# Decay attention and a gated convolution: one key tile transposed on TensorE, and another order of the same steps

## The chip, the cores and the metric

The kernel runs on one core of a Trainium2 chip. The metric is the device time of one execution in microseconds (us). Before the change it is 206.38 us (median of 3 runs, 206.31 to 206.44).

## The reference

There are two parts, in float32 throughout. The first is linear attention with a decay: 4 batches, 8 heads, 768 positions, head size 64. Written for blocks of 64 positions, with `Dmask[i,j] = lam**(i-j)` for j <= i:

```python
intra = (qb @ kb.T * Dmask) @ vb                  # inside a block
inter = (qb * lam**(pos+1)) @ kv_state            # what earlier blocks left
out   = intra + inter
kv_state = lam**64 * kv_state + (kb * lam**(63-pos)).T @ vb
```

Its output, laid side by side over the heads, is x, with 512 columns. The second part is `out = (sigmoid(conv5(x)) * (x @ w_val)) @ w_out`, where conv5 is a causal convolution of 5 taps for each column, and both matrices are 512 x 512.

## The kernel before

**Tiles.** Two batches go together, and 128 positions make a chunk, so there are 12 chunks (0 to 5 are the first pair of batches, 6 to 11 the second). Every chunk has two loads of 1 MB on SyncE's queue: `ld.i.0` brings q and k with head columns on the partitions (qT, kT; buffers lq0 to lq2), `ld.i.2` brings v and k with positions on the partitions (buffers lv0 to lv2).

**Steps of a chunk i.** `s.i` (TensorE): scores from kT and qT; chunks 0 to 2 have them in two halves, `s.i.0` and `s.i.1`. `m.i.*` (VectorE, DVE): scores times the decay mask, out of PSUM into buffer A. `ia.i` (TensorE): A times v into the PSUM tile xp; there is one such tile (xp0, two banks) for all chunks. `in.i` (TensorE): the share of the state. `kd.i`: k times its decay, in place in the lv tile, on ScalarE (ACT) for the chunks in K_ACT and on GpSimd (POOL) else. `st.i` (TensorE): k times v, into PSUM. `up.i` (DVE): the new state. `fd.i` (POOL): the faded state for the next chunk. `qd.i` (POOL): q times its decay. `x.i`, `xh.i` (ACT) and `xl.i` (DVE for chunks 0 and 1, POOL else): x out of xp, split in a high and a low part for the products of higher precision. xp0 comes free for the next chunk when these have read it.

**Steps of the second part.** `t.*`: the five taps (one on ACT, four on DVE), `sg`: the sigmoid, `v` and `V`: 12 matmuls each for x @ w_val, `ap`, `hh`, `hl`: the gate and the split of the product, `p`: x @ w_out, `ev`, `o`: out of PSUM and to memory.

**Weights.** w_val, w_out and conv_w come as 64-bit floats. `wv.0`, `wv.1`, `wo.0`, `wo.1` load 1 MB each and `cv` loads 20 KB; the steps `.e .n .s .w .v` (DVE), `.r .m .h` (ACT) and `.l` (POOL) make a high and a low 32-bit part of them. `dm` (DVE, L216) makes the decay mask, `dc` (ACT, L237) cuts it to blocks, `qe` (POOL) makes the decay of q. `f.0` (L206) is a matmul of zeros that computes nothing. Nine such matmuls of zeros (L188) stand at the start.

**Order.** ORDER is a list of all steps, written out. `Plan.run` issues them in that order; each engine runs its own steps one after the other, and SyncE issues the DMAs in that order too. A name after the colon is the buffer that a step takes.

Of the kernel before, what the change touches and what calls it, by code (L numbers as in the profile page):

```python
# [37 lines left out]
wv.0.1.w wv.0.1.v wv.0.1.h ld.3.2:lv1 wv.1.0.n s.2.0:s0 wv.1.1.e:val3 s.2.1:u1,u2 up.1.0 xh.1 wv.0.1.l v.0.1
m.2.0.0:A0 m.2.1.0 wv.1.0.m:u0 xl.1 wv.1.0.w wv.1.0.r hi.0 pb.0.0:val0 m.2.0.1:A1 wv.1.0.s cv.e qd.2.0:qd1 wv.1.0.v
qd.2.1 wv.1.1.n x.1 wv.1.1.r cv.r s.4.0:s0 cv.n v.1.0:u3 v.1.1 wv.1.0.h wv.1.1.s wv.1.1.m:u0 m.2.1.1 wv.1.1.w wv.1.1.v  # L40
ia.2.0:xp0 ia.2.1 wv.1.0.l cv.m m.4.1.0:A0 kd.2.0 wv.1.1.h fd.1.0 wo.0.0.n:val1 cv.s in.2.0 x.2:x1 pb.1.0:val2
wv.1.1.l m.4.0.0 st.2:u1 wo.0.0.e wo.0.0.r up.2.0 qd.4.0:qd0 cv.w cv.v xh.2:xs1 wo.1.1.e:val3 t.0.0.0:u2,g0 s.3.0:s0
xl.2.0 wo.0.0.m:u0 v.0.2:u3 m.3.0.0:A1 ld.6.2:lv2 v.0.3 pb.0.1 t.0.0.1 kd.3.0 t.0.0.2 xl.2.1 t.0.0.3 wo.0.0.w qd.4.1
ld.5.0:lq2 wo.0.0.s t.0.0.4 v.1.2:u1 sg.0.0 qd.3.1:qd1 v.1.3 v.2.2:u3 v.2.3 pb.1.1 wo.1.1.n fd.2.0 wo.0.0.v m.3.1.0
wo.1.1.m:u2 wo.1.1.r ld.6.0:lq0 st.3:u0,u1 wo.0.0.h qd.3.0 ia.3.0:xp0 in.3.0 wo.1.1.w wo.1.1.s wo.1.1.v wo.0.0.l hi.1
s.5.0:s0 kd.4.0 v.2.0:u2 up.3.0 in.3.1 wo.0.1.e:val1 wo.0.1.r fd.3.0 wo.1.1.h wo.0.1.n wo.0.1.m:u0 wo.0.1.s wo.1.1.l
up.3.1 fd.3.1 ia.3.1 v.2.1 x.3 xh.3 xl.3.1 ia.4.0:xp0 t.0.1.0:u1 ld.5.2:lv1 wo.0.1.w xl.3.0 pb.2.0:val3 m.5.1.0:A1
m.5.0.0 wo.0.1.v pb.2.1 wo.0.1.h wo.0.1.l s.6.0:s0 st.4:u0,u2 qd.5.1:qd1 kd.6.0 t.0.1.1 t.0.1.2 t.0.1.3 in.4.0 up.4.0
fd.4.0 t.0.1.4 sg.0.1 v.3.0:u3 kd.5.0 v.3.2:u0 qd.5.0 in.4.1 ia.4.1 ld.7.2:lv0 t.0.3.0:u1 t.0.3.1 up.4.1 t.0.3.2
x.4:x2 t.0.3.3 t.0.2.0:u2 kd.5.1 v.3.3 pb.3.1:val1 t.0.2.1 t.0.2.2 xh.4:xs0 ld.7.0:lq1 ia.5.0:xp0 in.5.0 t.0.2.3  # L50
fd.4.1 st.5:u0 up.5.0 v.3.1 pb.3.0 t.0.3.4 xl.4.1 in.5.1 sg.0.3 t.0.2.4 ap.1.0 ap.0.0 sg.0.2 ap.1.1 xl.4.0
wo.1.0.e:val2 wo.1.0.r v.4.0:u0 v.4.2:u3 wo.1.0.n wo.1.0.m:u1 ap.0.1 v.4.1 wo.1.0.s hh.1.1:hs0 wo.1.0.w pb.4.0:val0
hh.1.0 hl.1.1 wo.1.0.v m.6.1.0:A0 v.4.3 m.6.0.0 t.1.1.0:u2,g1 t.1.1.1 wo.1.0.h ia.5.1 st.6:u0,u1 up.6.0 x.5 s.7.0:s0
ia.6.0:xp0 hl.1.0 p.1.1.0.0:u0 t.1.1.2 hh.0.1:hs1 hh.0.0 t.1.1.3 pk.6 wo.1.0.l p.1.1.0.1 pb.4.1 qd.6.1:qd0 t.1.1.4
qd.6.0 t.1.3.0:u3 sg.1.1 t.1.3.1 t.1.3.2 t.1.3.3 t.1.3.4 ev.1.1.0:o0 o.1.1.0 xh.5 in.6.1 hi.2 ia.6.1 p.1.0.0.0:u2
fd.6.0 x.6:x0 t.1.0.0:u0 hl.0.0 sg.1.3 hl.0.1 p.1.0.0.1 up.6.1 ld.11.2:lv1 t.1.0.1 t.1.0.2 t.1.0.3 t.1.0.4
p.0.1.0.0:u1 ev.1.0.0:o1 p.0.1.0.1 t.1.2.0:u3 m.7.0.0:A1 t.1.2.1 t.1.2.2 t.1.2.3 m.7.1.0 sg.1.0 xl.5.0 p.0.0.0.0:u2
p.0.0.0.1 xl.5.1 v.5.0:u0 ld.8.0:lq2 t.1.2.4 ev.0.1.0:o2 o.1.0.0 xh.6:xs1 qd.7.0:qd1 t.2.3.0:u1,g0 v.5.1 ap.3.0
ld.8.2:lv2 ev.0.0.0:o0 sg.1.2 pb.5.0:val2 ap.3.1 ap.2.0 qd.7.1 kd.7.1 ia.7.0:xp0 in.7.0 kd.7.0 ap.2.1 hh.2.1:hs0
st.7:u2,u3 fd.6.1 v.5.2:u0 v.5.3 hh.2.0 t.2.3.1 t.2.3.2 up.7.0 s.8.0:s0 in.7.1 t.2.3.3 t.2.1.0:u2 t.2.3.4 hh.3.0:hs1  # L60
ia.7.1 hh.3.1 hl.2.0 sg.2.3 pb.5.1 p.2.0.0.0:u1 t.2.0.0:u0 t.2.1.1 ld.9.2:lv0 t.2.1.2 t.2.0.1 fd.7.0 up.7.1 hl.2.1
t.2.0.2 t.2.0.3 kd.8.0 p.2.0.0.1 ev.2.0.0:o1 t.2.0.4 sg.2.0 p.2.1.0.0:u3 kd.8.1 t.2.2.0:u1 t.2.1.3 p.2.1.0.1 t.2.1.4
o.2.0.0 sg.2.1 m.8.0.0:A0 o.0.0.0 t.2.2.1 t.2.2.2 t.2.2.3 t.2.2.4 ev.2.1.0:o1 o.0.1.0 ap.4.0 ap.5.0 ld.9.0:lq0 hl.3.1
hi.3 hl.3.0 x.7 p.3.0.0.0:u0 p.3.0.0.1 p.3.1.0.0:u2 t.3.0.0:u3,g1 xh.7 p.3.1.0.1 o.2.1.0 ia.8.0:xp0 sg.2.2 ap.4.1
t.3.0.1 hh.4.0:hs0 t.3.0.2 t.3.0.3 qd.8.1:qd0 fd.7.1 qd.8.0 in.8.0 ev.3.0.0:o0 hl.4.0 hh.4.1 hl.4.1 ev.3.1.0:o2
t.3.0.4 st.8:u1,u0 up.8.0 xl.6.0 ap.5.1 p.4.0.0.0:u2 m.8.1.0 t.3.1.0:u1 xl.7.1 p.4.0.0.1 fd.8.0 in.8.1 t.3.1.1 t.3.1.2
ia.8.1 t.3.1.3 ev.4.0.0:o1 o.4.0.0 ld.10.0:lq1 s.9.0:s0 m.9.1.0:A1 p.4.1.0.0:u2 sg.3.0 x.8:x1 p.4.1.0.1 xl.6.1
# [15 lines left out]
t.5.2.0:u3 o.8.0.0 apw.5.1 hhw.5.1:hs1 t.5.2.1 t.5.2.2 p.9.1.0.1 ev.9.1.0:o2 t.5.2.3 t.5.2.4 sg.5.2 o.7.1.0 V.5.0:u1
hlw.5.1:val1 V.5.3:u0 apw.5.0 o.9.1.0 apw.5.3 hhw.5.3 hlw.5.3:val3 p.8.1.0.0:u2 p.8.1.0.1 V.5.2:u3 hhw.5.0 ev.8.1.0:o0
o.8.1.0 hlw.5.0 p.10.1.0.0:u0 o.6.0.0 apw.5.2 hhw.5.2 hlw.5.2 p.11.1.0.0:u1 p.11.0.0.0:u2 p.11.0.0.1 ev.11.0.0:o2
o.11.0.0 p.11.1.0.1 ev.11.1.0:o0 o.11.1.0 p.10.1.0.1 ev.10.1.0:o1 o.10.1.0 p.10.0.0.0:u3 p.10.0.0.1 ev.10.0.0:o2
o.10.0.0 p.11.1.1.0:u2 p.11.1.1.1 ev.11.1.1:o0 o.11.1.1
# [815 lines left out]
```

## Time and profile before

| | |
|---|---|
| median of 3 runs | 206.38 us |
| the profiled execution's own time | 206.52 us |
| its span, first to last instruction | 204.7 us |
| TensorE (PE) busy | 197.6 us, 97% |
| DVE busy | 154.1 us, 75% |
| ACT, POOL busy | 114.3 and 115.4 us |
| read from HBM | 29.38 MB |

Times in the profile count from the first instruction, so a span is about 1.8 us shorter than the execution's own time. Busy time of PE overlaps between matmuls that follow each other, and the end of a matmul is modelled; how long a step holds TensorE is read from the start of one step to the start of the next. SPq are DMA issues of SyncE. In a row of the timeline the brackets give the engine's idle time before the row, and what ended it.

### The profile page before, as it was taken

The numbers are of one execution on the slowest core, as the hardware profiler recorded it, in microseconds if no ns is written. First come the engines' busy times: TensorE is split into PE (matmuls) and PEld (weight loads), VectorE is DVE, ScalarE is ACT, GpSimd is POOL, SyncE is SP. The second block draws the span as 40 slices with busy tenths as digits, with TensorE's granted clock in tenths as the row PEclk, the third lists the DMA queues.
The fourth block names the chain that finished last, engine by engine and source line by source line (L and its number), as shares of the span: only waits on it lengthen the run. The fifth ranks groups of instructions, "written<-read, shape, count | busy, mean of one in ns | idle before, by whom it ended". The sixth has DMA issues, their size and how long they took to land.

```text
span 204.7 us, 7451 instructions
## 1 busy us (share of the span) xinstructions
PE 197.6 (97%) x3312; PEld 171.6 (84%) x3312; DVE 154.1 (75%) x240; ACT 114.3 (56%) x218; POOL 115.4 (56%) x113
## 2 busy tenths in 40 slices
...
GB/s 175 426 429 419 422 424 423 421 360 27 195 51 362 8 3 118 373 232 3 297 297 29 203 400 122 3 3 152 8 106 0 0 3 102 102 51 14 93 127 78
DMA packets 7952, 36.15 MB, mean 177 GB/s; under 512 B 1136, under 2 KB 1392, under 8 KB 4336
## 3 DMA queue, kind: packets, MB, share of 16 engines
...
q8 instruction: 26, 0.43, 0.9%
q14 instruction: 6, 0.05, 0.1%
HBM read 29.38 MB, written 6.29 MB: 174 GB/s over the span
## 4 chain that ended last, share of the span: by engine, by line
PE 87%; DMA 9%; SPq 2%; issue 0%; ACT 0%; ACTq 0%
PE op L841 33%; PE vp L732 33%; DMA lq<-in_qkv 9%; PE xp L510 5%; PE s L470 5%; PE xp L547 5%; PE st L572 4%; SPq L337 1%; PE xp L525 1%; PE s L460 1%; PE st L564 1%; PE xp L536 1%; SPq L355 0%; PE so L460 0%; ACT o L848 0%
## 5 line engine op out<-in xcount | busy, mean ns | idle before, releaser
L706 DVE SCALAR_TENSOR_TENSOR acc<-x,conv_sb,acc 128x512 f32<-128x512 f32 x96 | 71.5, 753 | 7.8 <-ACT acc L704 5.7
L732 PE MATMUL vp<-x_hi,wv_hi 128*128 128x256 f32 (+1 forms) x144 | 47.1, 327 | 0.0
L732 PE MATMUL vp<-x_hi,wv_lo 128*128 128x256 f32 (+1 forms) x144 | 45.9, 319 | 0.3 <-POOL wv_lo L303 0.3
L732 PE MATMUL vp<-x_lo,wv_hi 128*128 128x256 f32 (+1 forms) x144 | 45.8, 318 | 0.0
L841 PE MATMUL op<-wo_hi,hs 128*128 128x512 f32 x96 | 30.4, 398 | 0.0
L848 ACT COPY o<-op 128x512 f32<-128x512 f32 (+1 forms) x25 | 14.3, 570 | 28.5 <-PE op L841 24.2
L732 PEld LDWEIGHTS vp<-x_hi,wv_hi 128*128 128x128 f32 x144 | 27.3, 190 | 2.8
L732 PEld LDWEIGHTS vp<-x_hi,wv_lo 128*128 128x128 f32 x144 | 27.4, 190 | 2.4 <-POOL wv_lo L303 0.5
L732 PEld LDWEIGHTS vp<-x_lo,wv_hi 128*128 128x128 f32 x144 | 27.4, 190 | 1.9
L677 POOL TENSOR_TENSOR x_lo<-x,x_hi 128x512 fp32r<-128x512 f32 x20 | 25.8, 1311 | 4.7 <-ACT x_hi L666 4.7
L584 POOL TENSOR_TENSOR sdec<-state,qdec_c 128x512 f32<-128x512 f32 x17 | 18.4, 1080 | 9.2 <-DVE state L581 9.2
L814 POOL TENSOR_TENSOR hs<-g,hs 128x512 fp32r<-128x512 f32 x12 | 15.4, 1294 | 13.6 <-ACT hs L803 13.6
L420 POOL TENSOR_TENSOR qd<-lq,qdec_c 128x512 f32<-128x512 f32 (+1 forms) x18 | 22.6, 1272 | 0.0
L841 PEld LDWEIGHTS op<-wo_hi,hs 128*128 128x128 f32 x96 | 17.7, 188 | 4.0
L841 PE MATMUL op<-wo_hi,h_hi 128*128 128x512 f32 (+1 forms) x52 | 20.0, 385 | 0.0
L841 PE MATMUL op<-wo_hi,h_lo 128*128 128x512 f32 (+1 forms) x52 | 19.6, 377 | 0.0
L704 ACT ACTIVATE acc<-x,conv_sb 128x512 f32<-128x512 f32 x24 | 16.7, 696 | 5.1 <-DVE state L581 3.6
L841 PE MATMUL op<-wo_lo,h_hi 128*128 128x512 f32 (+1 forms) x52 | 19.5, 375 | 0.0
L841 PE MATMUL op<-wo_lo,hs 128*128 128x512 f32 x48 | 18.9, 393 | 0.0
L803 ACT CAST h_hi<-vp 128x512 fp32r<-128x512 f32 x12 | 6.9, 587 | 21.0 <-DVE vp L778 21.0
L581 DVE TENSOR_TENSOR state<-st,sdec 128x512 f32<-128x512 f32 x17 | 11.7, 688 | 8.8 <-PE xp L547 6.4
L778 DVE TENSOR_TENSOR vp<-vp,g 128x512 f32<-128x512 f32 x12 | 8.3, 698 | 11.9 <-PE vp L732 11.9
...
## 6 DMA issues: line engine op xcount, KB each, us to landing
...
w_raw<-in_w_val SPq DMA_DIRECT2D x2, 1024.0 KB, 12.6
w_raw<-in_w_out SPq DMA_DIRECT2D x2, 1024.0 KB, 17.6
...
lam_bc<-in_lam SPq DMA_DIRECT2D x1, 4.0 KB, 1.6
```

What stands on the lines that cost most here:

```text
L420: nc.gpsimd.tensor_tensor(out=s["qd"][:, hs, ms], in0=lds[i]["qT"][:, u].rearrange("p h (m i) -> p h m i", m=2)[:, :, ms], in1=qdec[:, hs, ...
L470: nc.tensor.matmul(sp[b][rows(m), k, :], t["kT"][rows(b), u, h, ms], t["qT"][rows(b), u, h, ms], start=True, stop=True,)
L510: nc.tensor.matmul(s["xp"][rows(hh), b ^ m, b, g, :], lds[i]["v"][rows(m), b, h * D : (h + 1) * D], s["A"][rows(m), b, h, :], start=b == 0 ...
L581: nc.vector.tensor_tensor(out=state, in0=s["st"][m], in1=sdec, op=ALU.add)
L584: nc.gpsimd.tensor_tensor(out=sdec, in0=state, in1=qdec_c[:, :, n - 1 : n].to_broadcast([P, H, D]), op=ALU.mult)
L677: nc.gpsimd.tensor_tensor(out=s["x_lo"][:, ts], in0=s["x"][:, ts], in1=s["x_hi"][:, ts].bitcast(F32), op=ALU.subtract)
L704: nc.scalar.mul(to, src, w)
L706: nc.vector.scalar_tensor_tensor(out=to, in0=src, scalar=w, in1=to, op0=ALU.mult, op1=ALU.add)
L732: nc.tensor.matmul(to, w[:, ct, fs], xx[:, ct], start=n_mm == 0, stop=n_mm == 3 * NT - 1)
L814: (nc.vector if direct else nc.gpsimd).tensor_tensor(out=to, in0=x["h", j, fs], in1=x["to", j, fs].bitcast(F32), op=ALU.subtract)
L841: nc.tensor.matmul(s["op", b, j][:, cols], hh, w[:, ft, cols], start=ft == 0 and n == 0, stop=ft == NT - 1 and n == 2,)
L848: nc.scalar.copy(s["o", b, j][:, cols], s["op", b, j][:, cols])
```

## The change

**k of chunk 0.** `K_PE = (0,)` names the chunk whose k in the second layout is no longer loaded. `ld.0.2` brings v alone, 0.5 MB. A new step `tr.0` on TensorE makes k from kT: 16 matmuls, a 64x128 piece of kT as the weights and a 64x64 identity (`eye`, two small copies on ACT) as the moving operand, into a PSUM tile of the tag xp, so in xp0. `kd.0.0` now runs on ACT, reads that PSUM tile and writes k with its decay into the lv tile (8 instructions, one for each head); before, two instructions on POOL did it. v and k lie one after the other in the lv tile now, and not head by head beside each other.

**Order.** ORDER is another list of the same steps. The loads now come as ld.0.0, ld.0.2, cv, ld.1.0, wv.0, ld.1.2, ld.2.0, ld.4.0, ld.2.2, wv.1, wo.0, wo.1; before they came as ld.0.0, ld.0.2, wv.0, ld.1.0, ld.1.2, wv.1, ld.2.0, ld.4.0, cv, ld.2.2, wo.0. TensorE's first steps:

```
before: s.0.0 s.0.1 ia.0.0 ia.0.1 f.0 st.0 s.1.0 s.1.1 v.0.0 ia.1.0 ia.1.1 in.1.0 st.1
        s.2.0 s.2.1 v.0.1 s.4.0 v.1.0 v.1.1 ia.2.0 ia.2.1 in.2.0 st.2 s.3.0 | v.0.2 ...
after:  tr.0 s.0.0 s.0.1 ia.0.0 s.1.0 ia.0.1 st.0 s.1.1 f.0 ia.1.0 s.2.0 ia.1.1 in.1.0
        s.2.1 s.4.0 v.0.0 st.1 ia.2.0 ia.2.1 in.2.0 v.1.0 v.1.1 v.0.1 st.2 s.3.0 | v.1.2 ...
```

DVE's first steps after the mask:

```
before: m.0 (4 steps) wv.0.0.e wv.0.0.n wv.0.1.e wv.0.0.s .w .v xl.0 up.0.0 m.1 (4 steps) ...
after:  cv.n cv.e m.0 (4 steps) wv.0.0.e wv.0.1.n wv.0.0.n m.1.0.0 wv.0.0.s wv.0.1.e up.0.0
        m.1.1.0 xl.0 m.1.0.1 m.1.1.1 wv.0.0.w wv.0.1.w wv.0.0.v ...
```

The core of the diff:

```diff
-K_ACT = (1, 2, 3, 4, 6)
+K_ACT = (0, 1, 2, 3, 4, 6)
 X_DVE = (0, 1)
+K_PE = (0,)
...
+    eye = const.tile([P, D], F32, name="eye")
+    for b in range(NB2):
+        nc.scalar.copy(eye[rows(b)], ident[rows(b), rows(b)])
...
+            for part in ((0, 1),) if lo and i in K_PE else ((0, 2),):
+                def go(lo=lo, part=part, tile_of=tile_of, src=qkv[pair, c]):
+                    nc.sync.dma_start(tile_of()[:, slice(*part)], src[:, lo + part[0] : lo + part[1]])
...
+            if i in K_PE:
+                for h in range(H):
+                    nc.scalar.mul(kv[:, :, h], held[i]["kt"][:, :, h], k_mask[:, h])
+                return
...
+            def turn(i=i, s=s):
+                s["kt"] = bank("kt", [P, NB2, H, D], "xp")
+                for h in range(H):
+                    for b in range(NB2):
+                        nc.tensor.matmul(
+                            s["kt"][:, b, h], lds[i]["kT"][rows(b), h // HP, h % HP, :], eye[rows(b)],
+                            start=True, stop=True,
+                        )
```

The last steps of the two lists are alike: the end is the half-width `p.11.1.1`, its `ev` and its `o`.

## Rows read from the trace of the kernel before

**Rows 1.** The page's head, and its line of busy time for TensorE.

```profile
span 204.7 us, 7451 instructions
...
PE 197.6 (97%) x3312; PEld 171.6 (84%) x3312; DVE 154.1 (75%) x240; ACT 114.3 (56%) x218; POOL 115.4 (56%) x113
```

**Rows 2.** Busy by stretch: from:to, length, PE, PEld, DVE, ACT, POOL, clock, DMA, GB/s.

```profile
6.20:17.85 11.65, 10.20 (x142) 8.36 (x143) 9.31 (x17) 5.78 (x11) 6.07 (x7) 1.00 1.01 423
17.85:35.32 17.47, 16.95 (x389) 15.54 (x388) 16.34 (x32) 14.06 (x35) 9.55 (x9) 1.00 1.01 424
35.32:201.67 166.35, 166.25 (x2770) 143.77 (x2764) 124.57 (x184) 92.62 (x171) 95.89 (x86) 1.00 0.36 133
201.67:204.70 3.03, 0.00 (x1) 0.00 (x0) 0.00 (x0) 0.37 (x1) 0.00 (x0) 1.00 0.36 130
```

**Rows 3.** The chain of waits, 0 to 40 us: start, length, what.

```profile
4.34 18.07 DMA lq<-in_qkv
...
24.51 1.62 PE vp L732 x12
...
27.22 3.07 PE vp L732 x24
30.29 1.90 PE xp L525 x32
32.18 1.03 PE xp L536 x32
33.22 1.08 PE st L564 x32
```

**Rows 4.** Timeline of TensorE: start, length, line, operation, tiles, count, idle before.

```profile
6.21 1.16 PE L460 MATMUL s<-lq 64*128 64x128 f32 x16 [0.95 <-DMA lq<-in_qkv]
7.20 1.06 PE L460 MATMUL so<-lq 64*128 64x128 f32 x16
8.78 2.06 PE L525 MATMUL xp<-A,lv 128*64 128x128 f32 x32 [0.51 <-DVE A L483]
10.76 1.12 PE L206 MATMUL fill<-zero 128*128 128x512 f32 x2
12.04 1.15 PE L564 MATMUL st<-lv 128*64 128x64 f32 x32
13.64 1.16 PE L460 MATMUL s<-lq 64*128 64x128 f32 x16 [0.45 <-DMA lq<-in_qkv]
...
17.85 1.97 PE L525 MATMUL xp<-A,lv 128*64 128x128 f32 x32
...
22.45 1.16 PE L460 MATMUL s<-lq 64*128 64x128 f32 x16 [0.52 <-DMA lq<-in_qkv]
```

**Rows 5.** Timeline of DVE, same columns.

```profile
2.47 4.02 DVE L216 TENSOR_TENSOR_SCAN mask_c<-lam_bc,sdec 128x128 f32<-128x128 f32 x8 [1.46 <-DMA lam_bc<-in_lam]
7.42 1.29 DVE L483 TENSOR_TENSOR A<-s,mask_c 128x512 f32<-128x512 f32 x2 [0.93 <-PE s L460]
8.62 1.28 DVE L483 TENSOR_TENSOR A<-so,mask_c 128x512 f32<-128x512 f32 x2
11.16 0.43 DVE L261 TENSOR_SCALAR w_em<-w_raw 128x512 int32<-128x512 int32 x1 [1.26 <-DMA w_raw<-in_w_val]
11.51 0.42 DVE L268 TENSOR_SCALAR w_em<-w_raw 128x512 int32<-128x512 int32 x1
...
14.32 1.28 DVE L672 TENSOR_TENSOR x_lo<-xp,x_hi 128x512 fp32r<-128x512 f32 x2
...
33.15 1.31 DVE L261 TENSOR_SCALAR w_em<-w_raw 128x512 int32<-128x512 int32 x1
```

**Rows 6.** Timeline of ACT, same columns.

```profile
14.96 1.24 ACT L237 COPY dmask<-mask_c 64x512 f32<-64x512 f32 x2
...
17.71 2.45 ACT L401 ACTIVATE lv<-lv,mask_c 128x128 f32<-128x128 f32 x8 [0.42 <-DMA lv<-in_qkv]
```

**Rows 7.** Timeline of POOL, same columns.

```profile
32.89 1.28 POOL L303 TENSOR_TENSOR wv_lo<-w_em,wv_hi 128x512 fp32r<-128x512 f32 x1 [1.04 <-ACT wv_hi L299]
```

More of the change, by code (lines that the diff above doesn't have):

```diff
@@ L38 @@
[L38 to L67, printed above, removed]
@@ L83 @@
[L83 to L87, printed above, removed]
+qe ld.0.0:lq0 tr.0:xp0 dm.0 dm.1 s.0.0:s0 dc ld.0.2:lv0 kd.0.0 cv cv.n ld.1.0:lq1 wv.0:g0 cv.e qd.1.1:qd0 m.0.1.0:A0
@@ new lines @@
+s.0.1:u0,u1 m.0.0.0 m.0.0.1:A1 m.0.1.1 ld.1.2:lv1 wv.0.0.e:val0 wv.0.1.n:val1 wv.0.0.r ld.2.0:lq2 ld.4.0:lq0 wv.0.0.n
+ld.2.2:lv2 ia.0.0:xp0 s.1.0:s0 ia.0.1 xh.0:xs0 wv.1:g1 wo.0:hs0 x.0:x0 wv.0.1.m:u2 m.1.0.0:A0 wv.0.0.s hi.0 st.0:u3
+wv.0.1.e up.0.0 wo.1:hs1 qd.1.0 fd.0.0 s.1.1:u0,u1 f.0:u3 ld.3.0:lq1 m.1.1.0 xl.0 wv.0.1.r m.1.0.1:A1 ld.4.2:lv0
+m.1.1.1 wv.0.0.m:u3 kd.1.0 wv.0.0.w ia.1.0:xp0 qd.2.0:qd1 wv.0.1.w s.2.0:s0 ia.1.1 in.1.0 wv.0.0.v m.2.0.0:A0 qd.2.1
+wv.0.0.h cv.m s.2.1:u0,u1 xh.1 wv.0.1.s m.2.1.0 wv.0.1.v xl.1 s.4.0:s0 wv.0.1.h cv.r wv.0.0.l m.2.1.1:A1 v.0.0:u3
@@ new lines @@
+qd.4.0:qd0 m.2.0.1 st.1:u2 ld.3.2:lv1 x.1 wv.0.1.l ld.5.0:lq2 wv.1.1.n:val2 wv.1.1.e wv.1.0.n:val3 wv.1.1.r up.1.0
+wv.1.1.m:u0 ia.2.0:xp0 ia.2.1 wv.1.0.e wv.1.1.s in.2.0 wv.1.1.w wv.1.0.r wv.1.1.v wo.0.0.n:val0 wv.1.0.s wv.1.0.m:u1
+wv.1.1.h kd.2.0 v.1.0:u2 wv.1.0.w wv.1.0.v wv.1.0.h v.1.1 pb.1.0:val1 wv.1.1.l cv.s wv.1.0.l cv.w cv.v wo.0.0.e
+t.0.0.0:u0,g0 m.4.1.0:A0 fd.1.0 v.0.1 pb.0.0:val2 st.2:u1 m.4.0.0 wo.1.1.n:val3 up.2.0 ld.6.2:lv2 qd.4.1 wo.0.0.r
+s.3.0:s0 wo.0.0.m:u2 wo.0.0.w ld.6.0:lq0 x.2:x1 wo.1.1.e wo.0.0.s xh.2:xs1 xl.2.0 v.1.2:u3 v.1.3 pb.1.1 t.0.0.1
@@ new lines @@
+t.0.0.2 t.0.0.3 t.0.0.4 xl.2.1 fd.2.0 wo.0.0.v kd.3.0 qd.3.0:qd1 v.0.2:u1 v.0.3 m.3.0.0:A1 v.2.2:u3 qd.3.1 pb.0.1
+m.3.1.0 sg.0.0 wo.1.1.m:u2 wo.1.1.w ia.3.0:xp0 wo.1.1.r wo.1.1.s st.3:u1,u0 wo.1.1.v wo.0.0.h in.3.0 up.3.0 wo.0.0.l
+kd.4.0 s.5.0:s0 wo.0.1.e:val0 wo.0.1.r fd.3.0 wo.1.1.h v.2.0:u2 wo.0.1.n in.3.1 wo.0.1.s wo.0.1.m:u1 up.3.1 ia.3.1 x.3
+wo.0.1.w wo.1.1.l v.2.1 wo.0.1.v v.2.3 ia.4.0:xp0 m.5.0.0:A1 xh.3 pb.2.0:val3 qd.5.0:qd1 xl.3.0 t.0.1.0:u0 m.5.1.0
+ld.5.2:lv1 wo.0.1.h t.0.1.1 st.4:u1,u2 xl.3.1 in.4.0 pb.2.1 v.3.2:u3 t.0.1.2 t.0.1.3 v.3.3 fd.3.1 up.4.0 s.6.0:s0
@@ new lines @@
+in.4.1 kd.6.0 t.0.3.0:u1 t.0.1.4 sg.0.1 wo.0.1.l t.0.2.0:u0 t.0.3.1 ia.4.1 pb.3.1:val0 t.0.2.1 t.0.2.2 t.0.2.3 kd.5.0
+t.0.3.2 fd.4.0 up.4.1 x.4:x2 xh.4:xs0 m.6.1.0:A0 t.0.2.4 sg.0.2 ld.7.2:lv0 hi.1 qd.5.1 t.0.3.3 t.0.3.4 kd.5.1 m.6.0.0
+xl.4.0 sg.0.3 ld.7.0:lq1 xl.4.1 v.3.0:u3 v.3.1 fd.4.1 ia.5.0:xp0 in.5.0 pb.3.0 ap.1.1 hh.1.1:hs0 ap.1.0 ap.0.0
+wo.1.0.e:val1 wo.1.0.r st.5:u2 wo.1.0.n v.4.0:u0 up.5.0 ap.0.1 v.4.1 wo.1.0.s wo.1.0.m:u1 v.4.2:u3 v.4.3 hh.1.0 hl.1.0
+wo.1.0.w wo.1.0.v in.5.1 t.1.2.0:u2,g1 ia.5.1 pb.4.0:val2 t.1.2.1 pb.4.1 qd.6.0:qd0 s.7.0:s0 m.7.1.0:A1 x.5 st.6:u0,u1
@@ new lines @@
+up.6.0 hl.1.1 wo.1.0.h wo.1.0.l ia.6.0:xp0 p.1.1.0.0:u3 t.1.2.2 hh.0.0:hs1 hi.2 t.1.2.3 t.1.1.0:u0 qd.6.1 pk.6 xh.5
+p.1.1.0.1 ev.1.1.0:o0 t.1.1.1 hl.0.0 t.1.2.4 fd.6.0 t.1.1.2 in.6.1 up.6.1 sg.1.2 ia.6.1 kd.7.1 o.1.1.0 p.1.0.0.0:u3
+hh.0.1 hl.0.1 xl.5.0 p.1.0.0.1 t.1.1.3 t.1.1.4 t.1.3.0:u2 ld.8.0:lq2 ev.1.0.0:o1 xl.5.1 sg.1.1 t.1.3.1 t.1.3.2 kd.7.0
+fd.6.1 o.1.0.0 t.1.3.3 t.1.3.4 p.0.1.0.0:u1 t.1.0.0:u3 t.1.0.1 t.1.0.2 qd.7.0:qd1 p.0.1.0.1 v.5.0:u0 t.1.0.3 t.1.0.4
+sg.1.3 ld.8.2:lv1 x.6:x0 xh.6:xs1 p.0.0.0.0:u2 ev.0.1.0:o2 sg.1.0 v.5.1 pb.5.0:val1 qd.7.1 m.7.0.0 ap.2.1 hh.2.1:hs0
```

83 lines of the change are left out of this document (49 added, 34 removed).

## The prediction

> **What bounds the kernel now.** The page's busy line comes first: TensorE is busy 197.6 of 204.7 us, DVE 75%, ACT and POOL 56% each [rows 1]. A share of 97% says that time is lost in few places, so the next view is the busy time by stretch [rows 2]. From 35.32 us to the last matmul at 201.67 TensorE is busy 166.25 of 166.35 us: there it waits for nobody, and after it only the last copy and store follow, 3.03 us. In 17.85 to 35.32 it misses 0.52 us, in 6.20 to 17.85 it misses 1.45. In both of these early stretches the loads run without a pause, DMA share 1.01 at 423 and 424 GB/s. The granted clock is 1.00 in all four, the upper of its two levels. The timeline of TensorE then names the early waits [rows 4]: its first useful matmul stands at 6.21, when lq of chunk 0 has landed; then 0.51 for the first masked scores, 0.45 for lq of chunk 1 at 13.64, 0.52 for lq of chunk 2 at 22.45. The chain of waits says the same: one piece of 18.07 us, from the issue of chunk 2's lq, and from there matmuls alone [rows 3].
>
> So the kernel is a start bounded by loads and short chains, and then 166 us of TensorE at work. A change can win only what the start loses. It loses whatever TensorE work it adds, unless that falls into a wait, and whatever new wait the other order brings.
>
> **How I count.** Both orders have done the same TensorE steps when s.3.0 ends (the bar in the lists of the change), but for tr.0. Before, that is at 35.32. I follow the new order to this point, with start-to-start times of the rows, and leave the rest as it is unless something there comes late.
>
> **Loads.** lq of chunk 0 is still the first large load: 6.2. At 424 GB/s 1 MB (1.05 million bytes) takes 2.47 us. v alone is half of it: 7.4. cv has 20 KB, 0.05 us by its bytes; small pieces may cost more, and I take 0.1. Then lq of chunk 1 lands at 10.0 (13.6 before) and wv.0 at 12.5 (11.2 before, [rows 5]); lv of chunk 1 at 15, lq of chunk 2 at 17.4 (22.4 before).
>
> **tr.0.** 16 matmuls. Its weights have 128 columns like those of s, where 8 matmuls hold TensorE 0.99 us (6.21 to 7.20, [rows 4]), so 16 would take 1.98; it streams 64 columns like st, whose 16 matmuls take 1.08 [rows 3]. I take the middle, 1.5. The scores, not needed by it but queued behind it, start at 7.7 and end at 9.7. Their masks started 1.21 after them (6.21 to 7.42, [rows 4, 5]): 8.9; two take 1.28, so chunk 0's first pair is there at 10.2 and the second at 11.4.
>
> **kd.0.0 on ACT.** It stands behind dc, which can start when the mask is made at 6.49 [rows 5] and takes 1.24 [rows 6]: 7.8. tr.0 is done at about 7.9. Eight scalings take 2.45 [rows 6], there out of SBUF, here out of PSUM. As bounds I have dc's two copies of 512 columns, 1.24 for the same 1024 columns, and eight times its 0.62, 5.0; the nearest row is the eight scalings themselves, so 2.45, and kt has been read at 10.35. This matters because kt lies in xp0: ia.0.0 can't write there before. It starts at 10.4, a wait of 0.7 where the masks alone would allow 10.2. With 1.24 for kd nothing changes beyond that 0.2; with 5.0 everything to ia.1.0 shifts, and that one stands at 19.7 (below), 1.8 more. The two eye copies on ACT stand ahead of 6.2 in an engine that has nothing else: nothing. POOL loses two instructions, and no one waited for POOL there: nothing.
>
> Behind ia.0.0 (0.95, half of the 1.90 of [rows 3]) come s.1.0 (0.99, its lq is there), ia.0.1 (0.95), st.0 (1.08) and s.1.1 (0.99): 15.4.
>
> **The wait that takes over: DVE.** f.0 writes the bank of st.0 and must wait for up.0.0; ia.1.0 needs xp0, and must wait for xl.0, which reads it. Both are on DVE behind the first steps of w_val, and these start when wv.0 lands. Queue from 12.55: wv.0.0.e, wv.0.1.n, wv.0.0.n, m.1.0.0, wv.0.0.s, wv.0.1.e, up.0.0, m.1.1.0, xl.0. Four of the short ones at 0.34 (11.16 to 11.51), four at 0.60 (half of 7.42 to 8.62), and xl.0 1.28 [rows 5]: 5.04, so 17.6. st.0, s.1.0 and ACT's part (the relu, xh.0 behind ia.0.1 at 13.3) are there in time. To this I add 0.2: the row at 33.15 shows wv.*.e at 1.31 where the one at 11.16 takes 0.43, and POOL had an instruction running until 34.17 meanwhile [rows 5, 7]; here POOL has two scalings of q (I price each like that instruction, 1.28) from 10.0 to 12.6, the last beside wv.0.0.e. So xl.0 ends at 17.8 and ia.1.0 starts at 17.85; f.0 runs from 16.0 to 17.3 (1.28, [rows 4]), so TensorE waits 0.6 ahead of it and 0.5 behind it.
>
> The Trainium skill ("SBUF — State Buffer", section "SBUF: two separate sides") says that VectorE in a mode with two ports and GpSimd share a pair of ports as an exclusive lock, and that the loser is blocked for the other's whole instruction. The trace agrees (1.31 against 0.43). Without this rule the time would come out 0.2 lower, at 207.1.
>
> That 17.85 is when ia.1.0 starts before, too [rows 4]. The difference is that v.0.0 was done by then and now is not: 12 matmuls, 1.62 us when they stand alone between attention steps (v.0.1, [rows 3]). tr.0's own 1.5 us lie inside the waits: with 1.08 or with 1.98, ia.1.0 stays where DVE lets it.
>
> **From ia.1.0 to the end of s.3.0.** Before: 17.47 us, with 0.52 of waiting for lq of chunk 2 [rows 2, 4]. That wait goes, since s.2.0 comes at 18.8 and its load at 17.4. v.0.0 comes on top, 1.62. Against it, v.1.0, v.1.1 and v.0.1 now stand in one block and not in two, and a block's ends cost something: alone 1.62, in a pair 3.07/2 = 1.53 [rows 3]: some 0.15 less. So 17.47 - 0.52 + 1.62 - 0.15 = 18.4, and s.3.0 ends at 36.3, 0.9 later than before. What could be late in it: kd.1.0 and kd.2.0 on ACT, wv.0.0.l on POOL ahead of v.0.0; by the same rows all are there 0.8 us or more ahead.
>
> **Behind that.** 166.35 us and the end, 3.03, with the same steps [rows 2]. In this stretch TensorE can win 0.1 at most by what the rows show; the ends of matmuls are modelled, so waits under 0.2 may hide, and I allow 0.5. It can lose: on POOL wv.1.1.l, wv.1.0.l, fd.1.0 and qd.4.1 stand ahead of xl.2.0 and xl.2.1, six instructions of about 1.28 [rows 7], and wv.1.0.l waits for kd.2.0 on ACT. I get xl.2.1 done at 40.3 and v.2.2, which needs it, at 42. That is a margin of 1.7; others in a list of 700 steps are thinner.
>
> **Sum.** Span 17.85 + 18.4 + 166.35 + 3.03 = 205.6 against 204.7, so 0.9 more on the profiled execution's 206.52: 207.4. The median before is 0.14 below that execution: **207.3**.
>
> **Rivals.**
> - *Not slower: xp0 comes free before f.0 ends.* Place: ia.1.0. If DVE's queue takes 1.1 us less than I count, both waits at f.0 are gone and ia.1.0 starts at 16.75: 206.2. If ia.0.0 doesn't wait for kd.0.0 either, another 0.5: 205.7. For it: loads that TensorE waited for come 3.6 and 5 us earlier, and the waits for lq were most of what the start lost. Against it: nine DVE instructions between wv.0's landing and ia.1.0, each with a row. It decides at 17.3, the end of f.0. Chance of faster by over 0.2% (0.41 us; less than that this kernel's measurement can't tell from no change): 0.17.
> - *No change*: half of that gain, or hidden waits behind 35 us that the new order lacks: 206.4 to 206.8. Chance 0.25.
> - *Slower still: wv.0 lands late.* In the trace lv of chunk 1 landed 4.07 us behind lq of chunk 1 (13.64 to 17.71, [rows 4, 6]) where 1 MB takes 2.47: something holds the loads 1.5 us there, and the loads behind keep that. In the new order wv.0 lands at 12.5, ahead of that moment. If it comes sooner, as TensorE has 16 matmuls more to issue, DVE's queue starts at 14 and ia.1.0 stands at 19.3: 208.8. A stall of 1.3 (one POOL instruction) behind 36 us would give 208.6. Chance of both together 0.20.
>
> The forecast, 206.9 to 207.9, has 0.38. So slower by over 0.2% has 0.58, the same 0.25, faster 0.17. Range: 205.9 (the fast rival's middle) to 209.0 (the slow one's end, short of kd's upper bound with a stall).
>
> **What would show it.** Right: tr.0 of 1.1 to 2.0 us at 6.2; ia.0.0 at about 10.4 with ACT as the releaser; f.0 at about 16.0 and ia.1.0 at about 17.85, both released by DVE; no wait for lq at chunk 2's scores; s.3.0 ends at about 36.3, and behind it a TensorE without waits; 0.5 MB less read. Wrong: ia.1.0 ahead of 17.3 or behind 18.5; a wait for DMA at wv.0.0.e beyond 13; more than 0.5 us of TensorE idle behind 36 us.

## The result, and the profile after

207.7 us (median of ten executions, 207.34 to 209.16) against 206.34 for the kernel before on the same chip: ratio 1.0081, interval 1.0063 to 1.0098. Seven of the ten took 207.34 to 207.81 and three 209.07 to 209.16. The forecast was 207.3, slower, 205.9 to 209.0. So direction and size came out; the way there did not quite, as the stretches show. Ratios here and below leave out executions more than 1.5% above the fastest of their kernel, medians and ranges have all of them. The profiled execution took 207.62.

The head of the page, its busy line for TensorE, its line on HBM and the shares of the chain ([rows 1] has the first two of before):

```profile
span 205.8 us, 7534 instructions
...
PE 200.1 (97%) x3344; PEld 174.4 (85%) x3344; DVE 153.8 (75%) x240; ACT 117.0 (57%) x228; POOL 113.1 (55%) x111
...
HBM read 28.86 MB, written 6.29 MB: 171 GB/s over the span
...
PE 94%; DMA 3%; DVE 1%; issue 0%; ACT 0%; SPq 0%; ACTq 0%
```

The half megabyte is gone (29.38 MB before), and the piece of DMA in the chain has shrunk from 9% to 3%: in this chain TensorE and DVE set the start, and the loads hardly do. (How close the loads stand behind DVE, the experiments show.)

Busy time by stretch, cut at the same steps as [rows 2] (first useful matmul, ia.1.0, the end of s.3.0, last matmul), and below it the first stretch once more, cut where the granted clock changes:

```profile
6.45:18.53 12.08, 11.64 (x162) 10.11 (x163) 8.26 (x18) 7.61 (x18) 3.62 (x4) 0.86 1.00 408
18.53:37.15 18.62, 18.61 (x401) 16.97 (x401) 17.28 (x33) 14.91 (x37) 10.72 (x9) 1.00 1.01 425
37.15:202.79 165.64, 165.64 (x2770) 143.41 (x2764) 124.20 (x182) 92.25 (x170) 94.78 (x85) 1.00 0.36 127
202.79:205.85 3.06, 0.00 (x0) 0.00 (x0) 0.00 (x0) 0.37 (x1) 0.00 (x0) 1.00 0.35 129
...
6.45:8.47 2.02, 2.02 (x36) 2.02 (x38) 0.29 (x3) 1.23 (x2) 0.00 (x0) 1.00 0.93 320
8.47:11.88 3.41, 3.41 (x34) 3.19 (x34) 1.46 (x5) 2.18 (x8) 1.01 (x1) 0.50 1.01 425
11.88:18.53 6.65, 6.21 (x98) 4.90 (x99) 6.51 (x13) 4.20 (x8) 2.62 (x4) 1.00 1.02 426
```

s.3.0 ends at 37.15 instead of 35.32, 1.83 later (forecast: 0.9). From there TensorE needs 165.64 us instead of 166.35, 0.71 less (forecast: the same). Together 1.1 on the span. And from 8.47 to 11.88 the clock stood at the lower of its two levels, 1.2 GHz, which it never did in the trace of before, once it had risen at 5.22.

The timeline of TensorE, for [rows 4]:

```profile
6.45 2.00 PE L452 MATMUL kt<-eye,lq 64*128 64x64 f32 x32 [1.22 <-DMA lq<-in_qkv]
8.25 1.87 PE L490 MATMUL s<-lq 64*128 64x128 f32 x16
9.86 1.97 PE L490 MATMUL so<-lq 64*128 64x128 f32 x16
...
11.76 1.14 PE L555 MATMUL xp<-A,lv 128*64 128x128 f32 x16
...
15.87 1.16 PE L490 MATMUL so<-lq 64*128 64x128 f32 x16
16.96 1.12 PE L210 MATMUL fill<-zero 128*128 128x512 f32 x2
18.53 1.09 PE L555 MATMUL xp<-A,lv 128*64 128x128 f32 x16 [0.44 <-DVE x_lo L702]
```

tr.0 holds TensorE for 1.81 (6.45 to 8.25). ia.0.0 follows the scores with no wait at all; its releaser is neither ACT nor DVE, since the scores themselves were slow. f.0 follows s.1.1 without a wait of its own. ia.1.0 waits for x_lo. DVE, for [rows 5], shows the queue in front of that:

```profile
13.17 0.55 DVE L265 TENSOR_SCALAR w_em<-w_raw 128x512 int32<-128x512 int32 x1
13.64 0.75 DVE L272 TENSOR_SCALAR w_em<-w_raw 128x512 int32<-128x512 int32 x2
14.31 0.68 DVE L513 TENSOR_TENSOR A<-s,mask_c 128x512 f32<-128x512 f32 x1
...
15.99 0.69 DVE L609 COPY state<-st 128x512 f32<-128x512 f32 x1
...
17.20 1.28 DVE L702 TENSOR_TENSOR x_lo<-xp,x_hi 128x512 fp32r<-128x512 f32 x2
```

wv.0 landed at 13.15 and x_lo ended at 18.48. ACT, for [rows 6], scales k out of PSUM in 2.18 (2.45 out of SBUF before):

```profile
8.49 2.18 ACT L413 ACTIVATE lv<-kt,mask_c 128x128 f32<-128x128 f32 x8 [0.63 <-PE kt L452]
```

### The profile page after: what moved, and what is told of

Same layout as the page of the kernel before. It is cut to its first block, busy times and chain, and to the rows that moved or that the text cites. A ratio compares the mean times of both kernels' runs of the same rounds, so it can differ in the third digit from the quotient of the medians.

```text
span 205.8 us, 7534 instructions
## 1 busy us (share of the span) xinstructions
PE 200.1 (97%) x3344; PEld 174.4 (85%) x3344; DVE 153.8 (75%) x240; ACT 117.0 (57%) x228; POOL 113.1 (55%) x111
## 4 chain that ended last, share of the span: by engine, by line
PE 94%; DMA 3%; DVE 1%; issue 0%; ACT 0%; SPq 0%; ACTq 0%
PE vp L762 34%; PE op L871 33%; PE xp L540 5%; PE xp L577 5%; PE s L500 4%; PE st L602 4%; PE xp L555 3%; DMA lq<-in_qkv 3%; PE s L490 2%; PE st L594 2%; PE so L490 1%; PE xp L566 1%; PE kt L452 1%; DVE x_lo L702 1%; DVE state L609 0%; DVE A L513 0%
## 5 line engine op out<-in xcount | busy, mean ns | idle before, releaser
L736 DVE SCALAR_TENSOR_TENSOR acc<-x,conv_sb,acc 128x512 f32<-128x512 f32 x96 | 70.4, 753 | 5.5 <-ACT acc L734 3.4
L741 ACT ACTIVATE g<-acc 128x512 f32<-128x512 f32 x24 | 14.3, 599 | 16.6 <-DVE acc L736 16.6
L844 POOL TENSOR_TENSOR hs<-g,hs 128x512 fp32r<-128x512 f32 x12 | 16.2, 1352 | 9.5 <-ACT hs L833 9.5
L871 PEld LDWEIGHTS op<-wo_hi,hs 128*128 128x128 f32 x96 | 17.4, 188 | 3.9
```

The lines of the kernel that those rows point to most:

```text
L736: nc.vector.scalar_tensor_tensor(out=to, in0=src, scalar=w, in1=to, op0=ALU.mult, op1=ALU.add)
L741: nc.scalar.activation(xu[un]["g"][:, ct].rearrange("p u (b i) -> p b u i", b=NB2), xu[un]["acc", ct].rearrange("p b (u i) -> p b u i", u= ...
L844: (nc.vector if direct else nc.gpsimd).tensor_tensor(out=to, in0=x["h", j, fs], in1=x["to", j, fs].bitcast(F32), op=ALU.subtract)
L871: nc.tensor.matmul(s["op", b, j][:, cols], hh, w[:, ft, cols], start=ft == 0 and n == 0, stop=ft == NT - 1 and n == 2,)
```

## The experiments

Theory at the outset: tr.0 lies in a wait and costs nothing, DVE's queue behind wv.0 sets ia.1.0, and the fall of the clock is hidden in that. Rivals: the fall of the clock is the loss; the turning pays and the new order costs.

**More matmuls at the start, to hold the clock.**

```diff
-WARM = 9
+WARM = 14
```

> The changed kernel with 14 matmuls of zeros at the start and not 9, so that TensorE is busy until about 6.3 us. In the changed kernel's trace TensorE sat idle from 5.2 to 6.45, and the granted clock fell to its lower level at 8.47 and rose again at 11.88; s.0.0 and s.0.1 took 1.6 and 1.9 us and not 0.99. Theory A (the start is set by DVE's queue behind the landing of wv.0 at 13.15): the clock stays at its upper level, the scores are done by 10.3, but ia.1.0 still starts at 18.2 to 18.5; time 0 to 0.4 us below the changed kernel. Theory B (the lower clock sets the start): ia.1.0 at 17 or sooner, time 1.0 to 1.5 us below the changed kernel.

208.26 (ratio 1.0089, 1.0077 to 1.0101). The clock held; the scores took 0.95 each; ia.1.0 came at 18.38, still waiting for x_lo (0.67). So the clock does not set ia.1.0. But the time did not fall, it was 0.6 above the changed kernel's, which neither theory had, and the reason was new: s.4.0, 64 small matmuls in one burst, stopped for half a microsecond two matmuls ahead of its end, with nothing that it waited for. (Matmuls are counted here as the trace shows them: each matmul of the attention steps is two rows there, with a weight load for each.) The timeline of TensorE in this run:

```profile
23.86 1.16 PE L500 MATMUL s<-lq 64*64 64x64 f32 x62
25.52 0.27 PE L500 MATMUL s<-lq 64*64 64x64 f32 x2 [0.50 <-issue]
```

**The new order with k loaded.**

```diff
-K_PE = (0,)
+K_PE = ()
-tr.0:xp0
```

> The new order with the other part undone: k of chunk 0 is loaded again (K_PE empty, no tr.0), and kd.0.0 scales it in place on ACT. Theory A (the landing of wv.0 sets ia.1.0): that load is 0.5 MB longer, so wv.0 lands 1.2 us later, and the time is 0.8 to 1.4 us above the changed kernel. Theory B (tr.0, its ACT steps and the lower clock set the start): without them ia.1.0 comes sooner, and the time is 0.5 to 1.5 us below the changed kernel. Theory C (the new order alone is at fault, turning k is free): within 0.3 us of the changed kernel.

210.52 (1.0206, 1.0187 to 1.0225), 2.8 above the changed kernel and outside all three theories. wv.0 landed at 13.69, 0.5 later than with the turning and not 1.2, and TensorE shows the same two waits behind it, for the bank that f.0 writes and for x_lo:

```profile
17.07 1.12 PE L210 MATMUL fill<-zero 128*128 128x512 f32 x2 [1.41 <-DVE state L609]
18.86 1.09 PE L555 MATMUL xp<-A,lv 128*64 128x128 f32 x16 [0.67 <-DVE x_lo L702]
```

ia.1.0 starts 0.33 later than with the turning, so up to there the turning is worth no more than that in these two traces. s.3.0 ends 1 us later, 0.7 of it one more stop inside a burst; the rest of the loss was the same kind, stops of 0.4 and 1.2 us in steps that this edit does not touch.

**The old order with k turned.**

```diff
 ld.0.0:lq0
+tr.0:xp0
...
-kd.0.1
```

> The old order with k of chunk 0 turned by TensorE (tr.0 behind ld.0.0, kd.0.0 on ACT). Theory A: all loads behind the first come 0.5 MB, 1.2 us, sooner; tr.0 and the wait for kd.0.0 delay ia.0.0 by about 2 us (to 10.7), but v.0.0 waits for the split of w_val and the scores of chunk 2 for lq, and both come sooner: within 0.4 us of the kernel before, and 0.7 to 1.5 below the changed one. Theory B (turning k costs what the change cost): 0.9 to 1.5 us above the kernel before.

214.62 (211.33 to 219.24; ratio 1.0312, 1.0264 to 1.036), which neither theory had; the profiled execution took 212.73. The start is as theory A had it (s.3.0 ends at 35.44, before 35.32). What is lost is lost later, in in.4.0 above all:

```profile
54.35 0.55 PE L577 MATMUL xp<-qd,state 64*64 64x64 f32 x20
56.73 0.64 PE L577 MATMUL xp<-qd,state 64*64 64x64 f32 x11 [1.83 <-issue]
```

The stop itself costs 2 us. Right behind it the granted clock stood at the lower level, from 56.83 to 60.24, and there TensorE fell behind the kernel before by another 1.5 us. The stretch, in the columns of the busy time by stretch:

```profile
56.83:60.24 3.41, 3.41 (x24) 3.29 (x24) 1.37 (x3) 1.29 (x2) 2.46 (x3) 0.50 0.02 5
```

The executions of this kernel that took longest have the lowest mean clocks (0.974 to 0.984; 1.0 in the shortest), but only this one was profiled.

**Where these stops lie.** All of TensorE's instructions in the trace (matmuls, weight loads and the 40 to 44 of its sequencer), counted from the start, and the 26 packets of 16 KB of the instruction queue, give this for stops over 0.3 us inside a step (count of the first instruction behind the stop, its start, the start of the last packet due for it, the difference, the stop from start to start):

```
kernel                count            at     packet  diff  stop
before                 1985=193+7*256   53.24  50.94  2.30  0.32
14 first matmuls        705=193+2*256   25.52  23.18  2.34  0.72
k loaded                705=193+2*256   28.38  25.94  2.44  0.68
k loaded               3009=193+11*256  75.12  72.79  2.33  0.43
k loaded               5057=193+19*256 131.90 129.37  2.53  1.19
old order, turned      2241=193+8*256   56.73  54.47  2.26  2.05
old order, turned      2753=193+10*256  69.98  67.67  2.31  0.88
old order, turned      6081=193+23*256 153.60 151.17  2.43  0.61
```

Every one stands at the same place modulo 256, and 2.3 to 2.5 us behind a packet's start. Over all 14 traces of this study there are 350 such passings; none was crossed sooner than 2.21 us behind its packet. Most packets start behind the passing before: those with next to no load packets around about 0.7 us behind it, those with the queues full of loads about 2.8 (medians; where "full" begins moves the second by some 0.2). So, as an estimate from these sums (0.7 + 2.2 and 2.8 + 2.2), a stop needs 256 instructions that TensorE gets through in about 3 us (small matmuls alone), or in 5 while loads run. The Trainium skill ("Runtime: NRT & Kernel Launch", section "Instruction fetch mechanics") has the blocks of 256 instructions, refilled while the one before is executed, and calls the cost mostly hidden. The counts agree with the first, and the stops of 0.3 to 2 us are where the second does not hold. tr.0 adds 64 instructions ahead of everything (16 matmuls, each two rows and two weight loads), and so makes every passing fall 64 instructions earlier in the work. This was the theory for the next four runs, with the turning itself as the rival.

**The kernel before, with 64 instructions more and nothing turned.**

```diff
-WARM = 9
+WARM = 7
...
+    for _ in range(18):
+        nc.tensor.matmul(warm[:32, :8], zero[:, :32], zero[:, :8], start=True, stop=True)
```

> The kernel before, with nothing turned and its order untouched; only its 9 first matmuls on zeros become 7 of the same and 18 tiny ones (32 columns of weights, 8 moved), so that TensorE executes 64 instructions more ahead of s.0.0, as many as tr.0 adds, in the same idle time. Theory A (the holes marked 'issue' lie where TensorE's instruction stream passes from one block of 256 instructions to the next, and such a block comes by a packet of the instruction queue that was started too late): the passings fall 64 instructions earlier in the work, where they fell in the run with the old order and the turning; s.0.0 still starts at 6.2 to 6.4, in.4.0 gets a hole of 0.5 to 2 us, others follow; total 208 to 213. Theory B (the turning itself did it: the banks that it holds, ACT's multiplications by k's decay, the loads that shift): no holes, total 206.2 to 206.6.

212.02 (209.82 to 214.74; ratio 1.0239, 1.0197 to 1.0282), with no turning in it: theory A. The stop stands at the same count 2241, in in.4.0, behind the same 20 matmuls, and is as long:

```profile
54.09 0.55 PE L549 MATMUL xp<-qd,state 64*64 64x64 f32 x20
56.42 0.44 PE L549 MATMUL xp<-qd,state 64*64 64x64 f32 x11 [1.79 <-issue]
```

So this stop needs no turning: 64 instructions more ahead of it are enough. In the profiled execution (211.42) the span is 4.9 us longer than before. Three stops at passings make 3.5 of it: this one, one at 2753 in a v step (0.7 more than the same matmuls before) and one at 6081 (0.8 more). Another 1.2 is lost in st.8, most of it 0.67 of idle time that the profile puts down to a wait for ACT, in both runs; why ACT came late there was not followed up. The edit slowed the first scores too (1.87 and 1.84 us instead of 0.99 each), but s.3.0 ends at 35.19, 0.13 ahead of the kernel before, so nothing of the loss lies in the start.

**The old order, turned in 8 matmuls, the count nearly restored.**

```diff
-eye = const.tile([P, D], F32, name="eye")
+eye = work.tile([P, P], F32, name="eye", tag="o0", bufs=1)
...
-s["kt"][:, b, h], lds[i]["kT"][rows(b), h // HP, h % HP, :], eye[rows(b)],
+s["kt"][:, h], lds[i]["kT"][:, h // HP, h % HP, :], eye, start=True, stop=True,
...
-WARM = 9
+WARM = 4
...
+    wide = zero[:, None, :].to_broadcast([P, 4, C])
...
-        nc.tensor.matmul(warm, zero, zero, start=True, stop=True)
+        nc.tensor.matmul(warm, zero, wide, start=True, stop=True)
```

> The old order with k of chunk 0 turned, but in 8 matmuls (both halves at once, against a 128x128 identity) instead of 16, and with 4 wide matmuls on zeros (512 columns) for the 9 at the start: TensorE's instruction count ahead of s.0.0 is then 12 above the kernel before's, not 64. Theory A (holes at the block passings): the passings lie within 12 instructions of where the kernel before has them, in.4.0 takes 0.7 again, no hole over 0.5 us; tr.0 takes about 1.7 (16 passes of 53+53 ns), s.3.0 ends at 35.2 to 35.8; total 205.9 to 207.2. Theory B (the turning itself): in.4.0's hole stays, total 211 or more.

208.03 (206.69 to 208.15; 1.0073, 1.0054 to 1.0092). The profiled execution is the one of 206.69: no stop over 0.3 us, in.4.0 as before, tr.0 of 1.95 (0.25 more than expected), s.3.0 ends at 35.64, span 204.9 against 204.7. Theory A, for this execution. The other five took 207.84 or more, which it had not. Hence the same kernel once more:

> The same kernel as in the run with the old order and the turning in 8 matmuls, of which one execution took 206.7 and five 207.8 to 208.2: one more profiled execution, to see where the longer ones lose 1.3 us. Theory A: a block passing in a burst of small matmuls whose packet starts a little later than in the short execution, a hole 'issue' of 1 us or more at one place and the rest as it was. Theory B: the front (the loads land later, the clock rises later), the difference lies before 35 us.

208.46, and theory B: the clock rose at 6.45 and not at 4.50, the wide matmuls at the start lasted until after lq had landed (at 6.32), and tr.0 began 0.9 later. The first row is of the shorter execution, the others of the longer:

```profile
6.37 2.02 PE L451 MATMUL kt<-eye,lq 128*128 128x128 f32 x16
```

```profile
7.26 1.95 PE L451 MATMUL kt<-eye,lq 128*128 128x128 f32 x16
...
18.91 0.39 PE L760 MATMUL vp<-x_hi,wv_lo 128*128 128x256 f32 x1 [0.43 <-POOL wv_lo L307]
```

v.0.0 then lost another 0.75, on wv_lo, and the passing at count 2241 made a stop of 0.4, which is theory A's small share. This execution is longer than all six of the run before it, so for the five of 207.84 to 208.15 the cause is likely the same but not shown. Turning chunk 0's k in the old order is worth nothing even without stops: a span of 204.9 against 204.7 at best.

**The clock held without one instruction more.**

```diff
+    wide = zero[:, None, :64].to_broadcast([P, 3, 64])
...
-        nc.tensor.matmul(warm, zero, zero, start=True, stop=True)
+        nc.tensor.matmul(warm, zero, wide, start=True, stop=True)
```

> The changed kernel with its 9 first matmuls on zeros 192 columns wide instead of 128: TensorE is busy until about 6 us without one instruction more. Theory A (the hole of 0.5 us in s.4.0, in the run with 14 such matmuls, came from 20 instructions more, which moved a block passing into that burst; the clock itself is worth nothing because ia.1.0 waits for x_lo): the clock stays at its upper level, s.0.0 and s.0.1 take 0.95 each, s.4.0 takes 1.1 without a hole, ia.1.0 starts at 18.3 to 18.5 behind x_lo, v.1.2 at 36.9 to 37.2, total 207.0 to 207.5. Theory B (the hole comes from TensorE's being early there, or from the loads): the hole stays, v.1.2 at 37.8, total 208.0 to 208.4.

207.39 (1.0053, 1.0041 to 1.0065): theory A. The clock rose only at 6.77 and then stayed; ia.0.0 waits for its mask again, ia.1.0 for x_lo, and s.4.0 has no stop (compare the run with 14 first matmuls):

```profile
11.51 1.09 PE L556 MATMUL xp<-A,lv 128*64 128x128 f32 x16 [0.70 <-DVE A L514]
...
18.43 1.09 PE L556 MATMUL xp<-A,lv 128*64 128x128 f32 x16 [0.63 <-DVE x_lo L703]
19.69 1.16 PE L491 MATMUL s<-lq 64*128 64x128 f32 x16 [0.17 <-DMA lq<-in_qkv]
...
23.93 1.16 PE L501 MATMUL s<-lq 64*64 64x64 f32 x64
```

The scores are 1.5 us shorter, ia.1.0 is 0.1 earlier, and s.2.0 then waits for lq of chunk 2 and starts at 19.69, as late as in the changed kernel (19.64): the fall of the clock was hidden almost whole, and is worth 0.3 at most in the medians, at the edge of the two intervals.

**The kernel before with 12 instructions more.**

```diff
-WARM = 9
+WARM = 12
```

> The kernel before with 12 instead of 9 first matmuls on zeros: 12 TensorE instructions more, nothing else. Theory A (block passings): every passing falls 12 instructions earlier; the hole of 0.3 us in s.6.0 (at the passing at 53.24) is gone, as in the run with the turning in 8 matmuls, whose count is the same, and no other hole over 0.3 appears: 206.0 to 206.2, a version a little below both kernels. Theory B (the hole in s.6.0 has to do with the loads there, not with the count): 206.2 to 206.5, as before. A third outcome: the group of slow executions that the run with 8 matmuls had (208.0) belongs to this count, then about 207.7.

206.32 against 206.26 (1.0003, 0.9993 to 1.0012): the mechanism is theory A's, the time theory B's. The stop in s.6.0 is gone: from its start to st.4's it takes 1.31 in the kernel before (first row) and 0.98 here (second), while st.4 became 0.19 longer. Span 204.5 against 204.7, and nothing in the medians. None of the kernels here is faster than the kernel before.

```profile
52.11 1.51 PE L470 MATMUL s<-lq 64*64 64x64 f32 x63
```

```profile
51.91 1.16 PE L470 MATMUL s<-lq 64*64 64x64 f32 x64
```

**wv.0 loaded ahead of chunk 1's lq**, with 14 first matmuls.

```diff
+wv.0:g0
 ld.1.0:lq1
-wv.0:g0
...
-s.1.0:s0
...
-m.1.0.0:A0
...
 st.0:u3
+s.1.0:s0
 wv.0.1.e
 up.0.0
+m.1.0.0:A0
```

> As e1_warm14, with the load of wv.0 ahead of that of chunk 1's lq, and s.1.0 and m.1.0.0 behind st.0 and up.0.0. wv.0 lands at about 10.7 and not 13.15, so DVE's queue of w_val steps starts when the masked scores are done, at about 11.5. Theory A: ia.1.0 starts at about 17.3, and the time is 0.7 to 1.3 us below e1_warm14. Theory B (the landing of wv.0 does not matter): within 0.3 us of e1_warm14.

208.75 (1.0126, 1.0101 to 1.015), 0.5 above the run with 14 first matmuls and so outside both theories; ia.1.0 at 19.79 and not 17.3. wv.0 landed at 10.96, but DVE began with it at 12.50 and not at 11.5, behind chunk 0's masks, and then two of its steps took 1.62 and 1.49, while POOL scaled q, instead of 0.67 and 0.41 in the run with 14 first matmuls. DVE first, then POOL:

```profile
13.71 1.62 DVE L285 SCALAR_TENSOR_TENSOR w_em<-w_raw,w_em 128x512 int32<-128x512 int32 x1
15.26 1.49 DVE L265 TENSOR_SCALAR w_em<-w_raw 128x512 int32<-128x512 int32 x1
```

```profile
13.51 1.28 POOL L429 TENSOR_TENSOR qd<-lq,qdec_c 128x512 f32<-128x512 f32 x1 [7.28 <-DMA lq<-in_qkv]
...
14.80 1.67 POOL L429 TENSOR_TENSOR qd<-lq,qdec_c 128x512 f32<-128x512 f32 x1
```

That is the overlap of [rows 5, 7], twice; it cost 2 us here, and my expectation had left it out. That POOL is the reason rests on the overlap in time; no run here took POOL's steps away.

**x_lo ahead of two w_val steps**, the clock held as above.

```diff
 m.1.0.0:A0
+m.1.1.0
-wv.0.0.s
...
-wv.0.1.e
...
-m.1.1.0
 xl.0
-wv.0.1.r
...
+wv.0.0.s
 wv.0.0.w
+wv.0.1.e
+wv.0.1.r
```

> The kernel with the 192-column first matmuls (clock held, 207.39), and on DVE x_lo of chunk 0 taken ahead of two w_val steps (wv.0.0.s and wv.0.1.e, about 1 us together), which now follow chunk 1's masks; TensorE's instructions and their count are the same. Theory A (DVE's queue behind wv.0's landing sets ia.1.0, as the forecast said, but lq of chunk 2, landing at 19.6 and not at 17.4, stands right behind it): x_lo ends at 17.4 to 17.6, ia.1.0 starts at 17.8 when f.0 is done, s.2.0 then waits 0.6 to 0.8 for DMA lq and starts at 19.6 as before: total 207.2 to 207.5, no gain. Theory B (DVE's queue alone sets the front): s.2.0 starts at 19.0 and the total is 206.6 to 206.9.

207.72 (1.0065, 1.0051 to 1.0078): theory A, with 0.2 more than it had, as s.4.0 now waits 0.36 for a bank. DVE's queue does set ia.1.0, which moved from 18.43 to 17.81 with it; and the gain is gone one step later, at lq of chunk 2:

```profile
17.81 1.09 PE L556 MATMUL xp<-A,lv 128*64 128x128 f32 x16 [0.42 <-DVE x_lo L703]
19.63 1.16 PE L491 MATMUL s<-lq 64*128 64x128 f32 x16 [0.73 <-DMA lq<-in_qkv]
```

**The changed kernel, again**, unchanged, for an execution of the longer kind.

> The changed kernel itself, once more: of its ten executions seven took 207.3 to 207.8 and three 209.1, those three with a mean granted clock of 1.0, where most of the others have 0.992. If this one is long: theory A, the clock rises late (at 6.4 or later instead of 5.1), tr.0 and the first scores run at the lower level, and the loss is all before 20 us; theory B, it stays up, TensorE is earlier and a block passing makes a hole of 0.5 us or more in s.4.0 and others, as in the run with 14 first matmuls. If it is short: clock falls at about 8.5 for 3.4 us again.

> The same as the run before, for another chance to see a long execution; same expectations.

209.01 and 207.66. The second repeats the first profile. The first lost its time to the clock, in a third way: it rose at 3.95, TensorE stood idle for 1.82 us ahead of tr.0 (6.51), and the clock was down again from 7.37, ahead of most of tr.0, to 14.19.

```profile
7.37:14.19 6.82, 6.82 (x65) 6.59 (x65) 2.79 (x7) 2.62 (x9) 2.56 (x3) 0.50 1.00 420
```

ia.1.0 came at 20.24 there, 1.7 later; no stop at a passing. Its mean clock is 0.984 where the three long ones of the first ten have 1.0, so what lengthened those is still open.

## Why the prediction was right

**Right: what takes over.** The forecast said that the loads give way to DVE's queue behind wv.0, ending in x_lo ahead of ia.1.0. The queue was counted at 5.24 us and took 5.33 (13.15 to 18.48). Three runs with different clocks, counts and loads had the wait for x_lo at the same step, and the run that shortened the queue moved ia.1.0 by 0.6. But the margin is small: one step on, at s.2.0, lq of chunk 2 stands as close, and in the two runs that held the clock without shortening the queue s.2.0 waited 0.15 and 0.17 for it.

**Right: tr.0 is hidden.** 1.81 us, inside the bounds, and ia.1.0 starts where DVE lets it. That v.0.0 falls behind ia.1.0 and costs its 1.62 there is right as well: 18.62 us from ia.1.0 to the end of s.3.0, forecast 18.4.

**Two of its own signs of being wrong came, by little.** ia.1.0 started at 18.53 (the bound was 18.5), and wv.0.0.e began at 13.17, behind a landing later than 13. Both go back to one term:

**Mis-sized: when wv.0 lands**, 13.15 and not 12.5. lq came at 6.31 (+0.1); v alone took 1.66 and not 1.24; cv 0.32 and not 0.1; the two loads behind them 2.44 and 2.42, as counted. I had priced half a megabyte by its bytes, and 20 KB at little more. In the seven traces with these first loads the two together take 1.85 to 2.14, where the forecast had 1.34; why is not shown. With the 0.1 by which DVE's queue was longer and the 0.2 behind ia.1.0 this is the whole of the 0.9 by which the start was longer than forecast.

**Wrong, without effect: ACT releases ia.0.0; DVE releases f.0; lq of chunk 2 at 17.4.** The first two were covered by the slow scores: ia.0.0 stood at 11.76 and f.0 at 16.96, each without a wait. lq of chunk 2 landed at 19.59: I had seen the load that takes 4.07 in [rows 4, 6], counted its delay for the loads behind it in one rival, and left it out of this term. Here the load in question was that one itself (15.60 to 19.59). s.2.0 started at 19.64, so the forecast "no wait for lq" held only because ia.1.0 was late; the fast rival, ia.1.0 at 16.75, would have met this load and could not have had its 206.2.

**Not in it: the clock.** It was at the lower level from 8.47 to 11.88, after TensorE had stood idle for 1.22 us ahead of tr.0 (0.95 before, where it never fell). The scores took 3.5 us instead of 2.0, and that cost 0.3 at most.

**Not in it: the later stretch.** "Behind that unchanged" was 0.71 off, to the good: 0.33 is the stop in s.6.0, which the new order and count don't have; the rest is spread over many steps, none of them traced to a cause (when the stop alone went, in the kernel before with 12 instructions more, st.4 gave 0.19 of it back). I had looked for late producers there, and the thing to look at was how many instructions TensorE has had. The same term could have been 5 us to the bad, as the kernel before with 64 instructions more shows. That the forecast's total was 0.4 off and not more is partly luck: a start 0.9 too short against a rest 0.7 too long.
